# The ninth block's value products: two heads side by side instead of the same rows twice

## The chip, the cores and the metric

The kernel runs on one core of a Trainium2 chip. The metric is the device time of one execution in microseconds; less is better. The profile names the engines PE (TensorE's products), PEld (TensorE's loading of the stationary operand), DVE (VectorE), ACT (ScalarE), POOL (GpSimd) and SP (SyncE, which issues most transfers).

## The reference

Attention over 8 batches, 8 heads, 576 positions and 64 features, followed by a mixture of 8 experts in which each token is sent to one expert. Half of the heads see the last 32 positions, the other half every fourth of the last 128.

```python
scores = scale * np.matmul(q, k.transpose(0, 1, 3, 2))       # (8, 8, 576, 576)
scores = np.where(masks[None], scores, -1e9)                 # 32 allowed positions for each query
attn = np.exp(scores - scores.max(-1)); attn = attn / (attn.sum(-1) + 1e-9)
x = np.matmul(attn, v)                                       # -> (batch, position, 512)
# for each token: e = argmax(x @ w_gate), or the expert of the token before it where a local gate says so
out[b, s] = p[e] * (np.maximum(x[b, s] @ w1[e], 0.0) @ w2[e])
```

All of it is in float32.

## The kernel before

**Blocks.** The 576 positions are nine blocks of 64 queries (`QB`, `NB`). The queries of a block meet 96 keys (`KW`): their own 64 and the 32 before them. The dilated heads are put into the same form by an order of positions that the host applies. Heads go in pairs; there are 32 pairs (`NPB`), and each passes through the same steps.

**Steps of a pair n.** `scores(n)` writes masks and scores with keys on the partitions into two-bank PSUM tiles, in two units of five and four blocks; line 338 (DVE) applies the masks of the second unit, line 340 (ACT) takes the exponentials. `values(n)` multiplies the probabilities by the values, into which a column of ones is joined, so that column 64 of the 65 is the sum of the probabilities. A product has 96 contracted rows, 64 queries and 65 columns, and stands in one half of TensorE's columns: block 2k goes to PSUM partitions 0 to 63, block 2k+1 to partitions 64 to 127. Five slots (`SLOTS`) of two blocks are needed for nine blocks; in the last slot the second half repeats block 8 (`min(2 * k + h, NB - 1)`, line 383), so that all 128 partitions are written. `HALVES` splits the slots into two PSUM tiles `pv`, of two and three slots. For each tile DVE takes the reciprocals of the sums (line 389, into `rec`) and multiplies the 64 features by them (line 390, into `x`).

**Turning and storing.** Two pairs share a tile `x`. `turn(m)` transposes it for the routing: eight transposes of 128 positions (line 406) with two copies on ACT (line 407), then two of the 64 left over (line 410) and one copy (line 412), into `xt`. `store(m)` writes `x` to two tensors `xd` in DRAM, from which the experts later gather rows: one transfer for 512 positions (line 420) and one for the last 64 (line 422). `logits(g)` and the functions after it route a group of two batches on the basis of `xt`.

**Order.** PE, DVE, GpSimd and SP work in the order in which the program is written. In iteration n of the main loop: `scores(n)`, `share` (GpSimd copies the 32 overlapping rows of the values, line 276), a piece of routing work from the list `waiting` (`gap(SHARE)`), `values(n - 1)`, in odd iterations `turn((n - 3) // 2)`, another piece of routing work, then SP's loads for pair n + 3 (lines 264 and 269) and `store((n - 3) // 2)`. Routing work is taken from the list by a fixed credit and not by time. The tiles `pv`, `tp` and those of the routing share four PSUM banks (`banks`); scores have two tiles of two banks. Four sets of keys and values are held (`AHEAD`), three tiles `x`.

`paced(n)` lets GpSimd wait for a reciprocal of pair n before it gathers rows. `check()` looks, late in the expert stage, whether all of the reciprocals in `rec` lie between two bounds; if not, an exact version of the whole is run, which otherwise isn't.

**After attention** come the experts, 152 us to the end: products of weights (lines 923 to 1031), in which TensorE is fed by weights that SP loads one expert after the other.

Of the kernel before, what the change touches and what calls it, by code (L numbers as in the profile page):

```python
# [10 lines left out]
F32 = mybir.dt.float32  # L11
# [4 lines left out]
Alu = mybir.AluOpType  # L16
# [6 lines left out]
P = 128  # L23
B, H, S, DH = 8, 8, 576, 64
D = H * DH
# [7 lines left out]
QB = 64  # L33
NB = S // QB
# [3 lines left out]
NPB = B * NP  # L38
UNITS = ((0, 5), (5, 9))
SLOTS = (NB + 1) // 2  # L40
HALVES = ((0, 2), (2, SLOTS))
CB = 3
# [4 lines left out]
VW = DH + 1  # L47

CH = 2
# [165 lines left out]
def whole(ctx, tc, exact, bad, qk, v, wgl, w1, w2, con, adm, msk, qmk, out, cst, wg, ones, warm):  # L215
# [32 lines left out]
    def bank(shape, name):  # L248
        return banks.tile(shape, F32, name=name, tag="bank")

    rec = once.tile([P, NPB, SLOTS, 2], F32, name="rec")
    pace = once.tile([1, 2], F32, name="pace")
# [18 lines left out]
    def paced(n):  # L271
        nc.gpsimd.tensor_copy(pace, rec[:1, n, SLOTS - 1])

# [97 lines left out]
    def values(n):  # L371

        vt = loaded[n][2]
        if n % 2 == 0:
            xs[n // 2] = xp.tile([P, SLOTS, 2, 2, DH], F32, name="x")
        x = xs[n // 2]
        pr = prob.pop(n)
        for a, z in HALVES:
            pv = bank([P, z - a, 2, VW], "pv")
            for k in range(a, z):  # L380
                for u in range(2):
                    for h in range(2):
                        i = min(2 * k + h, NB - 1)
                        c, p = next((c, p) for c, p in reversed(pr) if c <= i)
                        nc.tensor.matmul(pv[h * QB:(h + 1) * QB, k - a, u], lhsT=p[:, u, (i - c) * QB:(i - c + 1) * QB],  # L385
                                         rhs=vt[:, u, i], start=True, stop=True, tile_position=(0, h * QB),
                                         skip_group_check=True)
            r = rec[:, n, a:z]
            nc.vector.reciprocal(r, pv[:, :, :, DH])
            nc.vector.tensor_tensor(x[:, a:z, n % 2], pv[:, :, :, :DH],  # L390
                                    r.unsqueeze(3).to_broadcast([P, z - a, 2, DH]), op=Alu.mult)
        del loaded[n]

    def turn(m):

        x = xs[m]
        b, g = divmod(m, 2)
# [5 lines left out]
        for c in range(CH):  # L403
# [3 lines left out]
            nc.scalar.copy(xt[:, g, c, s:s + full], tp.rearrange("p k t -> p (k t)"))  # L407
        tp = bank([P, CH, S - full], "tp")
        for c in range(CH):
            nc.tensor.transpose(tp[:, c], x[:S - full, S // P, c].rearrange("p u d -> p (u d)"),  # L410
                                ident[:S - full, :S - full])
        nc.scalar.copy(xt[:, g, :, s + full:s + S], tp)

    def store(m):

        x = xs.pop(m)
        b, g = divmod(m, 2)
        full = S // P * P
        to = xd[g][b * S:(b + 1) * S]
        nc.sync.dma_start(out=to[:full].rearrange("(k p) f -> p k f", p=P),  # L420
                          in_=x[:, :S // P].rearrange("p k g u d -> p k (g u d)"))
        nc.sync.dma_start(out=to[full:], in_=x[:S - full, S // P].rearrange("p g u d -> p (g u d)"))

# [716 lines left out]
    def check():  # L1140

        flat = rec.rearrange("p n k u -> p (n k u)")
        fine = stage.tile([P, D], F32, name="y", bufs=3)[:, :NPB * SLOTS * 2]
        nc.vector.tensor_scalar(fine, flat, 1.0 / HIGH, None, Alu.is_ge)
# [6 lines left out]
        all_fine = sm.tile([1, 1], F32, name="all_fine")  # L1151
        nc.vector.tensor_scalar(all_fine, lp, float(P * NPB * SLOTS * 2), None, Alu.is_lt)
        over = sm.tile([1, 1], F32, name="over_any")
# [133 lines left out]
```

## Time and profile before

| | us |
|---|---|
| median of 3 runs | 668.17 (665.80 to 672.63) |
| the profiled execution | 665.66 |
| its span, first to last instruction | 663.7 |
| first scores; first product of an expert | 6.9; 154.2 |

| engine | busy us | share of the span | instructions |
|---|---|---|---|
| PE | 648.9 | 98% | 6466 |
| DVE | 373.4 | 56% | 755 |
| POOL | 190.7 | 29% | 169 |
| ACT | 189.2 | 28% | 348 |

How to read it: a line of a group names the source line, the engine, the operation, the output and inputs, the partitions by elements, and after x the count; behind the bar are the busy time and the mean duration of one in ns. The groups' busy time is a union, so for products that overlap in the pipeline it is less than count by duration. In the order of time a line has the start, the busy length, and in brackets how long the engine had been idle and what ended it. The clock granted to TensorE was full in every slice (0.999 on average). A float32 product shows as two records, a transpose as one.

### The profile page before, as it was taken

The page shows a single profiled execution, that of the slowest core. Times are in us where ns is not written, and L with a number is a line of the kernel's source. Part 1 is how long each engine was busy: PE and PEld are TensorE (multiplying, and loading weights), DVE is VectorE, ACT ScalarE, POOL GpSimd, SP SyncE. Part 2 cuts the span into 40 slices and gives each one's busy share as a digit, 9 for nine tenths or more (in the row PEclk, how much of TensorE's full clock was granted, in tenths as well). Part 3 has the DMA queues.
Part 4 walks back from the last instruction along what each step waited for, and adds up shares of the span by engine and source line. Part 5 has one row for each costly group of instructions (what it writes and reads, how often), then busy time and mean ns, then how long its engine had stood idle before and what let it go on. Part 6 is the DMA issues. An engine that isn't in the chain of part 4 may idle for free. (4 is left out here: it accounts for less than half of the span.)

```text
span 663.7 us, 15298 instructions
## 1 busy us (share of the span) xinstructions
PE 648.9 (98%) x6466; PEld 570.0 (86%) x6466; DVE 373.4 (56%) x755; ACT 189.2 (28%) x348; POOL 190.7 (29%) x169
## 2 busy tenths in 40 slices
PE   8999999999999999999999999999999999999996
PEld 6988888887688999999599989998899989899893
DVE  3548678584596595373547382717464536547441
ACT  3544343442113331222213223231222222223210
POOL 3322212251025420222551253323144113050021
PEclk9999999999999999999999999999999999999999
DMA  8989899748205398484543456541045451453001
GB/s 317 304 308 317 275 287 312 244 142 317 120 33 191 104 422 332 175 290 169 208 150 132 162 191 226 236 164 48 14 177 214 177 218 61 158 192 144 1 33 49
DMA packets 29357, 126.38 MB, mean 190 GB/s; under 512 B 4221, under 2 KB 13789, under 8 KB 25312
## 3 DMA queue, kind: packets, MB, share of 16 engines
q1 hardware_dynamic: 22480, 106.10, 44.1%
q0 software_dynamic: 6800, 19.21, 8.5%
q8 instruction: 53, 0.87, 0.5%
q14 instruction: 24, 0.20, 0.1%
HBM read 142.07 MB, written 19.20 MB: 243 GB/s over the span
## 5 line engine op out<-in xcount | busy, mean ns | idle before, releaser
L977 POOL DMA_INDIRECT out_dram<-y,tok x36 | 57.4, 1595 | 290.9 <-DVE y L1046 121.0
L949 PE MATMUL hp<-xc,sum 128*128 128x128 f32 x720 | 85.6, 275 | 0.4 <-DVE sum L816 0.4
L949 PEld LDWEIGHTS hp<-xc,sum 128*128 128x128 f32 x720 | 82.8, 192 | 0.8 <-PE hp L949 0.5
L1031 PE MATMUL yp<-sum,hc 128*128 128x256 f32 x360 | 82.7, 379 | 0.0
L959 DVE TENSOR_TENSOR h<-hp,h 128x512 f32<-128x512 f32 x45 | 30.9, 690 | 90.8 <-PE hp L949 90.1
L1031 PEld LDWEIGHTS yp<-sum,hc 128*128 128x128 f32 x360 | 68.2, 190 | 9.6 <-ACT y L1039 0.3
L1046 DVE SCALAR_TENSOR_TENSOR y<-yp,gate,y 128x256 f32<-128x256 f32 x45 | 21.7, 482 | 75.1 <-issue 48.0
L276 POOL COPY vt<-vt 32x1040 f32<-32x1040 f32 x32 | 35.5, 1110 | 93.0 <-DMA vt<-in_v_dram 62.1
L949 PE MATMUL hp<-xe,raw 128*128 128x128 f32 x480 | 58.8, 276 | 0.0
L949 PEld LDWEIGHTS hp<-xe,raw 128*128 128x128 f32 x480 | 56.6, 192 | 1.8 <-issue 1.5
L1031 PE MATMUL yp<-raw,h 128*128 128x256 f32 x240 | 57.0, 380 | 0.0
L333 PE MATMUL two<-kq 64*96 64x64 f32 x1152 | 54.9, 245 | 0.0
L853 POOL DMA_INDIRECT xg<-xd,tok x40 | 45.7, 1143 | 27.6 <-PE hp L949 15.0
L333 PEld LDWEIGHTS two<-kq 64*96 64x96 f32 x1152 | 52.8, 162 | 0.0
L1031 PEld LDWEIGHTS yp<-raw,h 128*128 128x128 f32 x240 | 44.4, 190 | 5.5
L953 ACT COPY h<-hp 128x512 f32<-128x512 f32 x45 | 26.4, 587 | 79.2 <-PE hp L949 75.3
L960 ACT ACTIVATE h<-h 128x512 f32<-128x512 f32 x45 | 28.4, 632 | 67.2 <-DVE h L959 67.2
L853 POOL DMA_INDIRECT xg<-xd,pos x40 | 43.9, 1098 | 12.1 <-issue 11.1
L338 DVE SCALAR_TENSOR_TENSOR pr<-two,mk 96x512 f32<-96x512 f32 x32 | 21.9, 685 | 44.9 <-ACT pr L340 34.0
L385 PE MATMUL pv<-vt,pr 96*64 96x65 f32 x1280 | 44.6, 224 | 0.8 <-issue 0.8
L385 PEld LDWEIGHTS pv<-vt,pr 96*64 96x64 f32 x1280 | 40.0, 138 | 3.3 <-issue 1.5
L1039 ACT ACTIVATE y<-yp,gate 128x256 f32<-128x256 f32 x45 | 21.3, 476 | 55.8 <-PE yp L1031 48.5
(223 smaller groups left out, 1008.7 us busy)
## 6 DMA issues: line engine op xcount, KB each, us to landing
raw<-in_w_dram SPq DMA_DIRECT2D x48, 2048.0 KB
kq<-in_qk_dram SPq DMA_DIRECT2D x32, 592.0 KB
vt<-in_v_dram SPq DMA_DIRECT2D x32, 292.5 KB
xd<-x SPq DMA_DIRECT2D x16, 512.0 KB
raw<-in_w_dram SPq DMA_DIRECT2D x4, 512.0 KB
xd<-x SPq DMA_DIRECT2D x16, 64.0 KB
xg<-xd,tok POOLq DMA_INDIRECT x40, 3.2
xg<-xd,pos POOLq DMA_INDIRECT x40, 3.2
```

The costliest lines, as they stand in the source:

```text
L276: nc.gpsimd.tensor_copy(vt[:WIN, :, 1:], vt[QB:, :, :NB - 1])
L333: nc.tensor.matmul(sc[:KW, u, (i - a) * QB:(i - a + 1) * QB], lhsT=kt[h, i * QB:i * QB + KW], rhs=qt[h, i * QB:(i + 1) * QB], start=bool(a ...
L338: nc.vector.scalar_tensor_tensor(pr, sc[:KW, :, :w], -CEIL, mk[:, kind].unsqueeze(1).to_broadcast([KW, 2, w]), Alu.max, Alu.min)
L385: nc.tensor.matmul(pv[h * QB:(h + 1) * QB, k - a, u], lhsT=p[:, u, (i - c) * QB:(i - c + 1) * QB], rhs=vt[:, u, i], start=True, stop=True, ...
L853: nc.gpsimd.indirect_dma_start(out=x[:rows, g], out_offset=None, in_=xd[g] if units[u]["late"] else xd[g][:EARLY * GS], in_offset=bass.Ind ...
L949: nc.tensor.matmul(to[:, m], lhsT=a[:, m, kk], rhs=b[:, kk], start=first and m == 0 and kk == 0, stop=(kk == DK // 2 - 1), skip_group_chec ...
L953: nc.scalar.copy(at((0, 1, 3)[k]), of)
L959: nc.vector.tensor_tensor(at(k), of, at(k), op=Alu.add)
L960: nc.scalar.activation(at(k), at(k), Act.Relu)
L977: nc.gpsimd.indirect_dma_start(out=out, out_offset=bass.IndirectOffsetOnAxis(ap=of_unit(u, "tok", j), axis=0), in_=y, in_offset=None, boun ...
L1031: nc.tensor.matmul(to, lhsT=a[:, m], rhs=b[:, m], start=first and m == 0, stop=(m == FK // 2 - 1), skip_group_check=True)
L1046: nc.vector.scalar_tensor_tensor(at(k), of, of_unit(u, "gate", k // 2), at(k), Alu.mult, Alu.add)
```

## The change

The ninth block is no longer written twice. Its two heads stand side by side in the two halves of the columns: head 0 in partitions 0 to 63, head 1 in partitions 64 to 127, of one further column group in the second `pv` tile. So each pair has nine column groups of sums in place of ten, and 18 products in place of 20. What follows is fitted to that layout: `rec` has nine columns (`SUMS`); the last group is multiplied by its own instruction, which writes it twice, into both head positions of a part `end` of the tile `x`; `turn` transposes `end` with all 128 rows, and takes the two wanted quarters of the result by two copies; `store` writes the last 64 positions with one transfer for each head.

```diff
-SLOTS = (NB + 1) // 2
-HALVES = ((0, 2), (2, SLOTS))
+FULLS = S // P
+HALVES = ((0, 2), (2, FULLS))
+SUMS = NB
...
-    rec = once.tile([P, NPB, SLOTS, 2], F32, name="rec")
+    rec = once.tile([P, NPB, SUMS], F32, name="rec")
...
-        nc.gpsimd.tensor_copy(pace, rec[:1, n, SLOTS - 1])
+        nc.gpsimd.tensor_copy(pace, rec[:1, n, SUMS - 2:])
...
-            xs[n // 2] = xp.tile([P, SLOTS, 2, 2, DH], F32, name="x")
-        x = xs[n // 2]
+            x = xp.tile([P, 4 * (FULLS + 1) * DH], F32, name="x")
+            xs[n // 2] = (x[:, :4 * FULLS * DH].rearrange("p (k g u d) -> p k g u d", k=FULLS, g=2, u=2),
+                          x[:, 4 * FULLS * DH:].rearrange("p (g u d) -> p g u d", g=2, u=2))
+        x, end = xs[n // 2]
         pr = prob.pop(n)
+
+        def product(to, h, u, i):
+            c, p = next((c, p) for c, p in reversed(pr) if c <= i)
+            nc.tensor.matmul(to[h * QB:(h + 1) * QB], lhsT=p[:, u, (i - c) * QB:(i - c + 1) * QB],
+                             rhs=vt[:, u, i], start=True, stop=True, tile_position=(0, h * QB), skip_group_check=True)
+
         for a, z in HALVES:
-            pv = bank([P, z - a, 2, VW], "pv")
+            last = z == FULLS
+            w = 2 * (z - a)
+            pv = bank([P, w + last, VW], "pv")
             for k in range(a, z):
                 for u in range(2):
                     for h in range(2):
-                        i = min(2 * k + h, NB - 1)
...
+                        product(pv[:, 2 * (k - a) + u], h, u, 2 * k + h)
+            if last:
+                for u in range(2):
+                    product(pv[:, w], u, u, NB - 1)
-            r = rec[:, n, a:z]
-            nc.vector.reciprocal(r, pv[:, :, :, DH])
-            nc.vector.tensor_tensor(x[:, a:z, n % 2], pv[:, :, :, :DH],
-                                    r.unsqueeze(3).to_broadcast([P, z - a, 2, DH]), op=Alu.mult)
+            r = rec[:, n, 2 * a:2 * z + last]
+            nc.vector.reciprocal(r, pv[:, :, DH])
+            nc.vector.tensor_tensor(x[:, a:z, n % 2], pv[:, :w, :DH].rearrange("p (k u) d -> p k u d", u=2),
+                                    r[:, :w].rearrange("p (k u) -> p k u", u=2).unsqueeze(3).to_broadcast(
+                                        [P, z - a, 2, DH]), op=Alu.mult)
+            if last:
+                nc.vector.tensor_scalar(end[:, n % 2], pv[:, w:, :DH].to_broadcast([P, 2, DH]), r[:, w:], None, Alu.mult)
...
-        tp = bank([P, CH, S - full], "tp")
+        tp = bank([P, CH, P], "tp")
         for c in range(CH):
-            nc.tensor.transpose(tp[:, c], x[:S - full, S // P, c].rearrange("p u d -> p (u d)"),
-                                ident[:S - full, :S - full])
-        nc.scalar.copy(xt[:, g, :, s + full:s + S], tp)
+            nc.tensor.transpose(tp[:, c], end[:, c].rearrange("p u d -> p (u d)"), ident)
+        for u in range(2):
+            h = slice(u * DH, (u + 1) * DH)
+            nc.scalar.copy(xt[h, g, :, s + full:s + S], tp[h, :, h])
...
-        nc.sync.dma_start(out=to[full:], in_=x[:S - full, S // P].rearrange("p g u d -> p (g u d)"))
+        for u in range(2):
+            nc.sync.dma_start(out=to[full:].rearrange("t (g u d) -> t u g d", g=2, u=2)[:, u],
+                              in_=end[u * DH:(u + 1) * DH, :, 0])
...
-        fine = stage.tile([P, D], F32, name="y", bufs=3)[:, :NPB * SLOTS * 2]
+        fine = stage.tile([P, D], F32, name="y", bufs=3)[:, :NPB * SUMS]
```

## The prediction

> **What bounds the kernel now.** I read the page's busy shares first, then TensorE's waits, then the groups by shape, then the order of time in the attention stage, which is the only stage that the change touches (about 7 to 154 us of a span of 663.7).
>
> ```profile
> PE 648.9 (98%) x6466; PEld 570.0 (86%) x6466; DVE 373.4 (56%) x755; ACT 189.2 (28%) x348; POOL 190.7 (29%) x169
> L385 PE MATMUL pv<-vt,pr 96*64 96x65 f32 x1280 | 44.6, 224 | 0.8 <-issue 0.8
> ```
>
> TensorE is busy for 98% of the span, and its waits are few: the longest total that it waits for anything is 1.7 us. So what TensorE no longer does in attention brings the whole end forward, unless another engine is late there. The second line is the value products: 1280 records for 32 head pairs are 40 per pair, two for each of 20 float32 products. The page hides where VectorE is not at 56%. Two stretches show it, an ordinary turn (33.50 on) and one that routes tokens (55.10 on); columns after the length are PE, PEld, DVE, ACT, POOL, clock, DMA share, GB/s:
>
> ```profile
> 33.50:40.82 7.32, 7.32 (x173) 6.88 (x170) 3.90 (x11) 3.91 (x7) 2.09 (x2) 1.00 0.99 352
> 55.10:72.23 17.13, 15.96 (x347) 14.71 (x346) 16.20 (x45) 7.72 (x15) 5.45 (x4) 1.00 0.96 307
> ```
>
> In the first TensorE never pauses and VectorE has half its time free. In the second VectorE is busy 95% and TensorE loses 1.2 us. That difference decides this case.
>
> **TensorE: what goes.** The order of time in an ordinary stretch:
>
> ```profile
> 40.02 1.39 PE L385 MATMUL pv<-vt,pr 96*64 96x65 f32 x40
> 41.34 1.09 PE L406 MATMUL tp<-cst,x 128*128 128x128 f32 x8
> 42.36 0.33 PE L410 MATMUL tp<-cst,x 64*128 64x64 f32 x2
> 42.62 2.15 PE L439 MATMUL lp<-xt,wg 128*32 128x288 f32 x32
> ...
> 35.04 0.27 PE L410 MATMUL tp<-cst,x 64*128 64x64 f32 x1
> 35.05 0.33 PE L326 MATMUL two<-am 64*96 64x320 bf16 x1
> ```
>
> One product record lasts 0.22 us, so 40 in 1.39 us start (1.39-0.22)/39 = 0.030 us apart. The ninth block loses two products, four records: 4 x 0.030 = 0.119 us per head pair (unrounded spacing 0.0297), 32 times = **-3.8 us**. The rest of the 1.32 us to the next row is a tail that stays. That the two halves of the new pair keep this pace is read from the rows before: those too alternate between column halves.
>
> **TensorE: the turned remainder.** The two remainder transposes have 64 rows; they become 128x128 like the eight before them. Those start (1.09-0.28)/7 = 0.116 us apart. Now the ten take 41.34 to 42.62 = 1.28 us; ten alike take 9 x 0.116 plus the 0.20 us that follow the eighth now, 1.25. So nothing in a turn followed by other work. But in five turns (20, 27, 35, 108, 119 us) the small transposes run among the mask products of the next scores, as the last two rows show. There the turn from L406 to the next values takes 2.92 us (34.02 to 36.94); afterwards 1.25 plus an even turn's 1.76 (38.26 to 40.02) = 3.01. Five times 0.1 = **+0.5**. Bounds: -0.5 (0.03 saved in each of 16) to +1.6 (0.1 lost in each); I take the value counted by turn.
>
> The trace has 0.20 us between the eighth large transpose's start and the first small one, twice their pace. [...]
>
> **VectorE: what is added.** Durations by shape:
>
> ```profile
> L390 DVE TENSOR_TENSOR x<-pv,rec 128x384 f32<-128x384 f32 x32 | 17.8, 557 | 1.1
> L390 DVE TENSOR_TENSOR x<-pv,rec 128x256 f32<-128x256 f32 x32 | 13.6, 425 | 1.1
> L389 DVE RECIPROCAL rec<-pv 128x6 f32<-128x6 f32 x32 | 6.1, 191 | 0.4 <-PE pv L385 0.2
> L389 DVE RECIPROCAL rec<-pv 128x4 f32<-128x4 f32 x32 | 5.4, 168 | 0.0
> L998 DVE TENSOR_SCALAR y<-yp,gate x4: 349/351/479, 360.8 to 609.9; 128x128 f32<-128x128 f32 x3, 128x256 f32<-128x256 f32 x1
> ```
>
> The second multiplication shrinks from 384 to 256 elements: -0.132 us. Its reciprocal has 5 values in place of 6: -0.011. The new tensor_scalar writes 128x128 from PSUM with a scalar per partition; L998 is the same shape and operands: +0.350, and about 0.03 between two VectorE instructions. Together +0.237 us a head pair, 7.6 us in all. (Bounds of the new instruction: 0.255, L453's 96x108 without a scalar tensor, to 0.57, L503's slowest 12x96 beside a GpSimd copy; L998 matches in shape.)
>
> In ordinary turns the cover is VectorE's idle time ahead of L338, 1.1 to 4.5 us. In the routing stretches there is none:
>
> ```profile
> 66.75 0.56 DVE L390 TENSOR_TENSOR x<-pv,rec 128x384 f32<-128x384 f32 x1
> 67.22 0.94 DVE L573 TENSOR_TENSOR lane<-cst,lanes 96x768 f32<-96x768 f32 x1
> ...
> 69.66 0.42 DVE L390 TENSOR_TENSOR x<-pv,rec 128x256 f32<-128x256 f32 x1
> 70.23 0.30 PE L410 MATMUL tp<-cst,x 64*128 64x64 f32 x2 [0.92 <-DVE rec L389]
> ```
>
> TensorE waits for the multiplication at 69.66 to free a bank. Behind it are three head pairs (57.02, 61.21, 66.75) in a VectorE run with 0.13 us of idle time: 3 x 0.237 - 0.13 = +0.6 at that point, and the 4 x 0.119 = 0.5 that TensorE had gained since 55.10 are lost to the same wait. **+1.1.** The group from 93 to 112 us has 1.2 us of small VectorE gaps for four pairs' 0.95, but 0.8 of it comes from one TensorE pause at 102.7 that nothing explains: +0.3. The tail (143 to 152) ends on the last x: its path gains 0.24 from the pair before, loses 0.14 and adds 0.38, ends some 0.2 later, and two pairs' gain (0.24) is lost: +0.4. One more 0.1 for the third group near 111.
>
> **What is covered.** ACT gets a second remainder copy (L412's row: 0.28 us, 16 times). It lies ahead of the next exponentials, where ACT is idle 0.49 us in the tightest ordinary turn; without that cover the exponentials come 0.28 us later, at most 4.5 us in all. SP issues one more transfer a turn, 0.51 us by L422, ahead of the next key load; SP then waits for value products (L269, 59.8 us over 27 times). The stores become 256-byte pieces: 256 in place of 64 packets of 1 KB. By the trace's packets those last 46 ns, 512-byte ones 27, 64-byte ones 11. At 27 this is 256 x 27 - 64 x 46 = 4.0 us on 16 engines, 0.25 us a turn; at 46, 0.55. Bounds are 11 and 46 and I take 27, the nearest size. Keys (packets of 4,736 bytes) land 1.9 us or more ahead of their scores before the first store, 3.9 or more after it. So nothing. The check reads 288 reciprocals in place of 320, and the GpSimd pace copy waits for a reciprocal as before: nothing.
>
> [...]
>
> **The sum.** -3.8 + 0.5 + 1.1 + 0.3 + 0.4 + 0.1 = **-1.4 us**. The profiled execution took 665.66 us, 2 more than its span, so it would take 664.3. The runs' median is 668.17, 2.5 above; the change goes one for one to the end, since the expert stage too is TensorE's: 668.2 - 1.4 = **666.8**. That is no change that a measurement of this kernel would tell from none (about 1%, 6.7 us).
>
> **Rivals.**
> 1. *The gain arrives whole.* For it: TensorE waits little, and the wait at 70.23 follows a 1.05 us cast that a GpSimd copy had slowed, which need not recur. Then -3.8, 664.4.
> 2. *VectorE becomes the bound; slower.* A head pair inside a saturated run turns -0.119 into +0.237, a swing of 0.356. The net gain of 3.3 is gone at 3.3/0.356 = 9.3 of 32 pairs. My count above is about 6. VectorE has no gap over 0.5 us in 53-74, 93-115 and 140-152 and little in the two 7 us runs at 47 and 85: 16 pairs in all, which gives -3.3 + 16 x 0.356 = +2.4, 670.6. Against it: TensorE reads most of these results a turn later.
> 3. *The change does not do what it says on TensorE:* the four records were free beside their neighbours, and the pass keeps 1.3 us. Then only costs stay: +2.4 from the sum's other terms, 670.6. Against it: the even spacing of starts.
> 4. *Small packets bind.* DMA is already 96 to 99% busy in both stretches above. It decides when three stores eat the 3.9 us of lead, 1.3 us each: 0.19 + 1.3 = 1.49 us for 256 packets on 16 engines, 93 ns a packet, twice the 1 KB packet's 46. At 140 ns, +2.05 us a turn is 33 us of transfers against some 16 idle (11% of 146): +17 less the gain, some 682.
>
> **Chances.** Forecast 0.52, rival 1 0.16, rival 2 0.18, rival 3 0.08, rival 4 0.06. None but rival 4 leaves the 1%; the runs spread 6.8 us, which gives 0.04 for faster and 0.02 more for slower. So 0.04, 0.88, 0.08. The range holds rivals 1 to 3 and reaches 2.4 us below and 1.4 above them for the spread of the runs: 662.0 to 672.0.
>
> **What would show it.** L385 with 36 records and about 1.27 us a pass; ten equal transposes; L998's kind of row in values at 0.35 us, 32 times; VectorE up about 7.6 us; a longer wait of the transposes near 70 us. Wrong if the stage's end (now 154.2) moves by more than 4 us, if TensorE begins to wait for VectorE in ordinary turns, or if keys land late.

## The result, and the profile after

The changed kernel took 667.69 us (median of 22 runs, 664.97 to 675.34), the kernel before 666.15 (22 runs beside it). The ratio is 1.001, with a 95% interval from 0.9992 to 1.0028: 0.5 us faster to 1.9 us slower, no change that counts. The forecast of no change holds, but its ratio, 0.998 (1.4 us faster), lies just outside the interval. The profiled execution took 668.03 us with a span of 666.2. In some runs the clock granted to TensorE is lower on average and the run is up to 15 us longer (e3's slowest, 681.11 at 0.977, beside 666.38 at full clock); where a text below says "at full clock", only runs with a mean granted clock of 0.997 or more are in the median (a run with one fall of 3.4 us in attention still counts: e11's profiled one has 0.997): 667.04 for the change (19 runs) and 666.09 for the kernel before (20; its clocks are not on record, and the two runs near 672.6 are left out by their time), 0.95 us slower.

The page of the changed kernel, its span, its busy shares and the value products:

```profile
span 666.2 us, 15143 instructions
...
PE 647.0 (97%) x6338; PEld 567.3 (85%) x6338; DVE 376.3 (56%) x787; ACT 192.9 (29%) x364; POOL 187.5 (28%) x169
...
L384 PE MATMUL pv<-vt,pr 96*64 96x65 f32 x1152 | 40.9, 225 | 0.3 <-issue 0.3
```

There are 128 value records fewer, 36 per pair in place of 40, each as long as before. Yet the span is 2.5 us longer. The attention stage, from the first scores to the first product of an expert, went from 147.30 (6.89 to 154.19) to 148.09 (6.89 to 154.98): +0.79. The rest of the span, from there to TensorE's last product, went from 503.23 to 504.79. The clock has no part in these 1.6 us: in both traces it falls only behind that last product, at 662.4 and 662.7 us. Waits make 1.0 of it, 0.57 us for a gather of rows of `xd` and 0.48 for ACT. For that gather e1, e3, e9 and e11 wait 0.46 to 0.57 us too, and the kernel before, e2, e4 and e10 wait 0 to 0.19; so the change may have a small part in the expert stage, which no run took apart.

What is to be explained is the stage: +0.79 where -1.4 was forecast, near the 0.95 at full clock. The +0.79 itself holds some luck. Each trace has a pause of TensorE that nothing releases (last section): it lengthens a pass of values by 1.07 us in the kernel before and by 0.57 in the changed one. Without the two the difference would be +1.3 (an estimate).

The groups by shape, with mean durations in ns behind the comma:

```profile
L400 DVE TENSOR_TENSOR x<-pv,rec 128x256 f32<-128x256 f32 x64 | 27.2, 425 | 2.2
L404 DVE TENSOR_SCALAR x<-pv,rec 128x128 f32<-128x128 f32 x32 | 10.9, 342 | 0.0
L399 DVE RECIPROCAL rec<-pv 128x5 f32<-128x5 f32 x32 | 5.9, 184 | 0.0
L426 ACT COPY xt<-tp 64x128 f32<-64x128 f32 x32 | 8.3, 261 | 2.2 <-PE tp L423 1.9
L423 PE MATMUL tp<-cst,x 128*128 128x128 f32 x32 | 6.5, 284 | 4.6 <-DVE rec L399 3.5 <-ACT xt L420 1.0
```

The added multiplication (L404) takes 0.342 us; 0.350 had been taken from L998. The durations of VectorE's instructions in the stage add up to 115.8 us in place of 108.6, 7.2 more. Its busy time rose by less than half of that, from 99.3 to 102.4 us (on the page from 373.4 to 376.3), since the records overlap: behind a multiplication of `pv` the next instruction starts 0.08 us before the end. The last line is where the time went: the remainder transposes now wait 3.5 us for VectorE's reciprocals and multiplications. TensorE's waits say how often:

```profile
PE tp L423 <- DVE rec L399: 3.5, 4, 1.2
...
PE kp L562 <- DVE x L400: 0.6, 1, 0.6
PE tp L884 <- DMA xg<-xd,tok: 0.6, 1, 0.6
PE hp L939 <- ACT le L459: 0.5, 1, 0.5
PE yp L1047 <- ACT y L1055: 0.5, 1, 0.5
```

Before, the first of these was one wait of 0.9 us, the second one of 0.4, and the others did not exist. The third and the last lie in the expert stage. Laid out along the stage, with a stretch measured from the start of one pass of values to the start of another:

| stretch | before | after | difference | forecast |
|---|---|---|---|---|
| first scores to the first pass | 4.47 | 4.61 | +0.14 | 0 |
| pairs 0 to 9 (ordinary turns) | 39.10 | 38.23 | -0.86 | -0.9 |
| pair 10 (turn at 51 us) | 4.64 | 5.63 | **+1.00** | -0.1 |
| pairs 11 to 14 | 17.14 | 17.33 | +0.20 | +0.6 |
| pairs 15 to 18 | 20.96 | 20.76 | -0.20 | -0.5 |
| pairs 19 to 22 | 17.58 | 17.25 | -0.33 | -0.1 |
| pairs 23 to 27 | 24.40 | 24.10 | -0.30 | -0.4 |
| pair 28 (turn at 136 us) | 4.77 | 5.47 | **+0.70** | -0.1 |
| pairs 29 to 31, to the first expert | 14.25 | 14.70 | +0.45 | 0.0 |

The forecast column is the prediction's sum, shared out by place. In pairs 0 to 9, where nothing waits, the sum is right to 0.1 us; in pairs 15 to 18 it is 0.3 too good. The row of pairs 19 to 22 holds both pauses: without them it would be about +0.2 (an estimate), since the turn at 107 us now waits 0.59 us for VectorE. The sum fails most at two single turns that it had counted as covered, and at the stage's end. The order of time in the first of them, in the changed kernel (start, length, and in brackets the idle time before it):

```profile
49.73 1.27 PE L384 MATMUL pv<-vt,pr 96*64 96x65 f32 x36
...
49.79 0.42 DVE L400 TENSOR_TENSOR x<-pv,rec 128x256 f32<-128x256 f32 x1
50.13 0.34 DVE L404 TENSOR_SCALAR x<-pv,rec 128x128 f32<-128x128 f32 x1
50.39 0.68 DVE L339 SCALAR_TENSOR_TENSOR pr<-two,mk 96x512 f32<-96x512 f32 x1
50.93 1.09 PE L419 MATMUL tp<-cst,x 128*128 128x128 f32 x8
...
51.11 1.05 POOL L277 COPY vt<-vt 32x1040 f32<-32x1040 f32 x1 [3.45 <-PE pv L384]
51.26 1.10 DVE L502 TENSOR_TENSOR_SCAN run<-row 12x96 f32<-12x96 f32 x1
...
52.47 0.42 DVE L400 TENSOR_TENSOR x<-pv,rec 128x256 f32<-128x256 f32 x1
...
53.04 0.41 PE L423 MATMUL tp<-cst,x 128*128 128x128 f32 x2 [1.01 <-DVE rec L399]
```

and in the kernel before:

```profile
50.26 0.56 DVE L390 TENSOR_TENSOR x<-pv,rec 128x384 f32<-128x384 f32 x1
50.73 0.68 DVE L338 SCALAR_TENSOR_TENSOR pr<-two,mk 96x512 f32<-96x512 f32 x1
...
51.60 0.34 DVE L486 TENSOR_TENSOR_SCAN run<-row 12x96 f32<-12x96 f32 x1
...
51.86 1.05 POOL L276 COPY vt<-vt 32x1040 f32<-32x1040 f32 x1 [4.25 <-PE pv L385]
```

Before, the scan starts 0.26 us ahead of GpSimd's copy and takes 0.34. In the changed kernel the copy starts first, 0.15 ahead, and the scan takes 1.10. The copy starts when the pass of values ends (51.85 before, 51.00 after), so TensorE's own gain brings it forward by 0.75; the scan comes forward by only 0.34. VectorE's queue there begins 0.62 earlier than before (the masks, 46.80 and 46.18), and loses 0.15 at L479, which takes 0.40 us in place of 0.25 beside the copy of the pair before, and 0.12 to the new multiplication. These 0.12 are seen in the rows: from the start of the second multiplication to that of the masks it is 0.47 us before (50.26 to 50.73) and 0.60 now (49.79 to 50.39). With the reciprocal, which is a little shorter, it is 0.121 us (0.696 and 0.817, the medians of the pairs in which VectorE goes on without a gap). Behind the scan stand the multiplications that free the PSUM bank for L423. At 136 us the copy is first in both kernels: 0.85 ahead of the scan before, which takes 0.41, and 0.43 ahead in the changed one (135.88 and 136.31), where the scan takes 0.82.

The end of the stage:

```profile
152.31 2.15 PE L455 MATMUL lp<-xt,wg 128*32 128x288 f32 x32
154.53 0.40 ACT L459 COPY le<-lp 128x288 f32<-128x288 f32 x1 [1.31 <-PE lp L455]
154.98 1.35 PE L939 MATMUL hp<-xe,raw 128*128 128x256 f32 x5 [0.52 <-ACT le L459]
```

The first expert product waits for ACT's copy of the last logits, which it doesn't read; before it followed the logits without a gap (152.11 to 154.19). That the two tiles got the same PSUM bank in the changed program and different ones in the one before is a guess; no trace shows the banks. The wait is there in e1, e5 and e12 too, and in none of the other runs below.

### The profile page after: what moved, and what is told of

Read it like the earlier page. It is cut to its first block, busy times and chain, and to the rows that moved or that the text cites. A ratio compares the mean times of both kernels' runs of the same rounds, so it can differ in the third digit from the quotient of the medians.

```text
span 666.2 us, 15143 instructions
## 1 busy us (share of the span) xinstructions
PE 647.0 (97%) x6338; PEld 567.3 (85%) x6338; DVE 376.3 (56%) x787; ACT 192.9 (29%) x364; POOL 187.5 (28%) x169
## 2 busy tenths in 40 slices
DMA packets 32686, 126.38 MB, mean 190 GB/s; under 512 B 8573, under 2 KB 17117, under 8 KB 28640
## 5 line engine op out<-in xcount | busy, mean ns | idle before, releaser
L993 POOL DMA_INDIRECT out_dram<-y,tok x36 | 55.4, 1539 | 295.4 <-DVE y L1062 124.1
L975 DVE TENSOR_TENSOR h<-hp,h 128x512 f32<-128x512 f32 x45 | 30.9, 690 | 90.9 <-PE hp L965 90.9
L384 PE MATMUL pv<-vt,pr 96*64 96x65 f32 x1152 | 40.9, 225 | 0.3 <-issue 0.3
L384 PEld LDWEIGHTS pv<-vt,pr 96*64 96x64 f32 x1152 | 36.4, 138 | 2.8 <-issue 0.9
```

What stands on the lines that cost most here:

```text
L384: nc.tensor.matmul(to[h * QB:(h + 1) * QB], lhsT=p[:, u, (i - c) * QB:(i - c + 1) * QB], rhs=vt[:, u, i], start=True, stop=True, tile_posi ...
L975: nc.vector.tensor_tensor(at(k), of, at(k), op=Alu.add)
L993: nc.gpsimd.indirect_dma_start(out=out, out_offset=bass.IndirectOffsetOnAxis(ap=of_unit(u, "tok", j), axis=0), in_=y, in_offset=None, boun ...
```

## The experiments

Theory A: the gain is eaten where GpSimd's copies slow VectorE's instructions, and would be whole without them. Theory B: VectorE's load as such, where it runs without a gap, makes TensorE wait. The times, each beside the kernel before on the same chip; "full clock" is the median at full clock less that of the kernel before, with the number of runs; "stage" is the attention stage of one profiled execution, "VectorE" the sum of the durations of its instructions there:

| run | time | ratio to before, 95% | full clock | stage | VectorE |
|---|---|---|---|---|---|
| before | | | | 147.30 | 108.6 |
| the change | 667.69 | 1.0010 [0.9992, 1.0028] | +0.95 (19) | 148.09 | 115.8 |
| e1_act9 | 665.86 | 0.9986 [0.9966, 1.0007] | -1.1 (11) | 146.21 | 104.6 |
| e2_before_dose | 673.22 | 1.0116 [1.0067, 1.0166] | +1.7 (1) | 150.49 | 120.0 |
| e3_after_dose | 672.14 | 1.0023 [0.9978, 1.0067] | -0.6 (5) | 154.72, clock | 127.6 |
| e4_once | 665.64 | 0.9994 [0.9968, 1.0019] | -1.3 (10) | 147.25 | 107.3 |
| e5_after_ns | 668.74 | 0.9983 [0.9958, 1.0009] | -0.4 (12) | 146.57 | 111.6 |
| e6_before_ns | 668.04 | 0.9997 [0.9985, 1.0008] | -1.1 (11) | 145.74 | 105.2 |
| e7_after_vf | 674.04 | 1.0085 [1.0062, 1.0108] | (0) | 152.62, clock | 113.0 |
| e8_act9_vf | 670.98 | 1.0022 [0.9998, 1.0045] | -1.7 (2) | 149.46, clock | 105.2 |
| e9_after_late | 665.60 | 0.9987 [0.9964, 1.0009] | -1.2 (10) | 146.50 | 115.8 |
| e10_before_late | 666.26 | 1.0002 [0.9979, 1.0026] | -1.6 (9) | 146.54 | 108.5 |
| e11_act9_late | 664.67 | 0.9986 [0.9971, 1.0000] | -2.0 (10) | 145.86, clock | 105.2 |
| e12_two_copies | 669.91 | 1.0031 [1.0002, 1.0060] | +1.1 (9) | 148.48 | 115.1 |

In the stages marked "clock" the granted clock fell to half on the way. A single stage also holds pauses of TensorE that lengthen it by up to 1.3 us and differ from trace to trace (last section), so stages less than about 1 us apart say little without the stretches behind them.

### e1_act9: the ninth multiplication on ACT

```diff
-                nc.vector.tensor_scalar(end[:, n % 2], pv[:, w:, :DH].to_broadcast([P, 2, DH]), r[:, w:], None, Alu.mult)
+                nc.scalar.activation(end[:, n % 2], pv[:, w:, :DH].to_broadcast([P, 2, DH]), Act.Copy, scale=r[:, w:])
```

> The changed kernel, with the ninth block's multiplication on ACT in place of VectorE (an activation with the reciprocal as its scale); nothing else differs. Theory 1, VectorE: the 3.8 us that TensorE saves are real and are lost only where VectorE's added 0.34 us a pair stands in a run without gaps. Then VectorE has 0.14 us a pair less than in the kernel before, TensorE's waits for it fall to or under those of before, and the time is 2.5 to 3.5 us under the kernel before (ratio 0.995 to 0.996). Theory 2, the rest of the change: full-height transposes, the second ACT copy and the 256-byte stores eat the gain. Then the time stays within 1 us of the kernel before, as the change has it, or above it, since ACT gets about 9 us more.

The stage is 1.9 us shorter than the changed kernel's and 1.1 shorter than before's; the time is 0.9 us under before by the ratio (interval 2.3 under to 0.5 over) and 1.1 at full clock. Right in direction, though the interval reaches past 0, and under half in size. The two turns make up the 1.9: pair 10 takes 4.52 in place of 5.63, pair 28 4.74 in place of 5.47; the other stretches differ by -0.23 to +0.46 and cancel. In the order of time the scan is ahead of the copy again:

```profile
50.22 0.35 DVE L502 TENSOR_TENSOR_SCAN run<-row 12x96 f32<-12x96 f32 x1
...
50.48 1.05 POOL L277 COPY vt<-vt 32x1040 f32<-32x1040 f32 x1 [3.64 <-PE pv L384]
```

What is still lost has other owners: the wait at the stage's end is the same, a turn at 104 us waits 1.1, and the last pair now reaches its values before GpSimd has copied them:

```profile
PE tp L423 <- DVE rec L399: 1.9, 2, 1.1
...
PE pv L384 <- POOL vt L277: 0.8, 1, 0.8
```

### e2_before_dose and e3_after_dose: one more multiplication per pair

Each adds, behind the second multiplication, a spare one of the added kind, whose result nobody reads; here in the changed kernel, and alike in the kernel before:

```diff
+                spare = work.tile([P, 2, DH], F32, name="spare")
+                nc.vector.tensor_scalar(spare, pv[:, w:, :DH].to_broadcast([P, 2, DH]), r[:, w:], None, Alu.mult)
```

> The kernel before, with the one VectorE instruction that the change adds (a tensor_scalar of 128x128 from PSUM with a reciprocal as its scalar) put behind the second multiplication of every pair, into a spare tile that nobody reads. VectorE has 0.37 us a pair more, 12 us in all; products, transposes and stores are as before. Theory 1: the time grows by 3 to 6 us (ratio 1.005 to 1.009), as waits of TensorE in the four routing groups. Theory 2: VectorE has the room, under 1 us.

The stage went from 147.30 to 150.49, +3.2. A pause in the pass at 89.7 us that nothing released makes 1.3 of it, but the pause of the kernel before, 1.07, is missing; so some 3.0 is left (an estimate), at the low end of what was expected, where the one run at full clock has +1.7. The passes of values kept their 1.32 us, so VectorE's load alone brings waits like those of the change:

```profile
PE tp L414 <- DVE rec L389: 3.3, 4, 1.3
```

Before there was 0.9 of them. Pair 10 alone loses 0.89, and there the scan meets the copy:

```profile
51.85 1.05 POOL L276 COPY vt<-vt 32x1040 f32<-32x1040 f32 x1 [4.06 <-DMA vt<-in_v_dram]
51.88 1.23 DVE L490 TENSOR_TENSOR_SCAN run<-row 12x96 f32<-12x96 f32 x1
```

The ratio, 1.0116, is mostly that of runs with a fallen clock, five of six; what that has to do with the waits is told in the last section.

> The changed kernel with its added VectorE instruction issued twice, the second time into a spare tile that nobody reads: 0.37 us a pair more again. Theory 1: 4 to 7 us above the changed kernel (ratio to the kernel before 1.006 to 1.011), more per dose than in the kernel before since TensorE is shorter. Theory 2: under 1 us above the changed kernel.

The stage rose by 6.6, and that number must not be taken as it stands. The stretches of 5 us from 70 us on (the last three columns are granted clock, DMA share and GB/s):

```profile
70.00:75.00 5.00, 3.75 (x42) 3.36 (x42) 3.64 (x9) 1.76 (x5) 0.87 (x1) 0.64 0.91 332
75.00:80.00 5.00, 5.00 (x51) 4.88 (x50) 2.43 (x7) 0.63 (x1) 0.17 (x1) 0.50 0.30 90
80.00:85.00 5.00, 5.00 (x87) 4.80 (x85) 1.07 (x3) 0.91 (x2) 1.04 (x1) 0.84 0.26 105
```

(1 - 0.64) + (1 - 0.50) + (1 - 0.84) = 1.02 times 5 us are 5.1 us of clock, so that about 1.5 is left, 1.2 of it in the same stretches. The five runs at full clock are 0.6 under the kernel before beside them, where the change is 0.95 over its own. So at full clock 11.8 us more of VectorE's durations on top of the change cost between nothing and 1.5 us: a miss for 4 to 7. The median of all 12 runs, though, is 4.9 over the kernel before; seven of them are not at full clock. In pairs 0 to 9 the stretch is the same to 0.01 us. Theory B, read as a price per us of load, falls, as far as the clock is full. What the load did bring is one wait of 2.67 us, from 68.6, right ahead of the clock's fall.

### e4_once: the ninth block written once

The whole second tile of sums is multiplied by one instruction of 128x320 (0.49 us), and the remainder is turned by eight products in column halves:

```diff
-                nc.vector.tensor_scalar(end[:, n % 2], pv[:, w:, :DH].to_broadcast([P, 2, DH]), r[:, w:], None, Alu.mult)
...
+            nc.vector.tensor_tensor(x[:, n % 2, 2 * a:2 * z + last], pv[:, :, :DH],
+                                    r.unsqueeze(2).to_broadcast([P, w + last, DH]), op=Alu.mult)
...
-            nc.tensor.transpose(tp[:, c], end[:, c].rearrange("p u d -> p (u d)"), ident)
+            for u in range(2):
+                h = slice(u * DH, (u + 1) * DH)
+                nc.tensor.matmul(tp[h, c], lhsT=x[:, c, SUMS - 1], rhs=ident[:, h], start=True, stop=True,
+                                 tile_position=(0, u * DH), skip_group_check=True)
```

> The ninth block's heads side by side as in the change, but written once: a tile of nine column groups for each pair, so that one multiplication of 128x320 takes the ninth group too (about 0.49 us, against 0.557 before and 0.425 + 0.342 in the change), and the remainder is turned by four products with a half of the identity, each in its half of the columns, which gives the layout of before and needs one ACT copy. The stores are smaller still: 1024 packets of 512 bytes and 256 of 256 a turn, four transfers. Theory 1: VectorE has 0.07 us a pair less than before, TensorE keeps its 3.8 us and loses at most 0.1 us a turn on eight records in place of two; 2 to 4 us under the kernel before (ratio 0.994 to 0.997). A rival, small packets: the same time as the kernel before or above it.

A miss: VectorE is down to 107.3, under before's 108.6, and the stage is still 147.25, the time within the interval of no change. A turn takes 1.02 + 0.38 us, where the changed kernel's takes 0.93 + 0.31 to 0.40; a pause of 1.0 in the pass at 32.0 us is in it (the kernel before's trace has one as long), and pair 28 lost 0.74 to a wait for VectorE: there the scan starts 0.24 behind the copy and takes 1.01. So a lighter VectorE does not do it by itself: it depends on where its instructions fall. At full clock the time is 1.3 under before. The stores of this kernel have the smallest pieces of all, and in attention no product waited for a transfer.

### e5_after_ns and e6_before_ns: without GpSimd's copies

Both leave out the copies from pair 4 on, as told in the expectation; their routing differs from the reference's, so they are read against each other:

```diff
-            share(k)
+            if k < AHEAD:
+                share(k)
```

> The changed kernel without the GpSimd copies of the overlapping value rows from pair 4 on (the rows of an earlier pair stay in their place, so values and routing are not the reference's; the check's verdict is set to 'fine' so that the exact version isn't run). To be read against e6, which has the same data. Theory A, collisions: in the traces so far every VectorE instruction of attention that lasts 0.1 us longer than its shortest like stands beside one of these copies (4.4 us of lengthening in the changed kernel, 3.3 before). If that is what ate the gain, the attention stage (first scores to first expert product) is 2.5 to 3.5 us shorter here than in e6. Theory B, VectorE's plain load and place in the order: the stage here is within 1 us of e6, or longer.

> The kernel before, without the same copies and with the same check left out; the partner of e5. Theory A: the stage is 1 us shorter than the 147.3 of the kernel before at most, since TensorE waits little there, and 2.5 to 3.5 us longer than e5. Theory B: within 1 us of e5.

Without the copies both stages are about 1.5 us shorter. The difference between the layouts is the same as with them, +0.83 against +0.79 (at full clock 0.7 and 0.95), and not 2.5 to 3.5 the other way, so Theory A falls as an account of the whole sum. But the sum hides three parts. Pairs 10 and 28 differ by +0.09 and +0.05 in place of +1.00 and +0.70: their loss is gone with the copies. The pauses differ: e6 has none, and e5 has one like the changed kernel's; without them the layouts would differ by +1.3 with the copies and +0.3 without (estimates), so that the like size of +0.79 and +0.83 is partly chance. And up to the last logits the changed layout is 0.74 us ahead. It is given back, and more, at the stage's end, where the wait for ACT's copy has grown:

```profile
PE hp L939 <- ACT le L459: 1.5, 1, 1.5
```

### e7_after_vf and e8_act9_vf: values' multiplications ahead of routing

The first piece of routing work goes behind the values in place of ahead of them, so that the bank is freed earlier; e8 has the multiplication of e1, too.

```diff
-        gap(SHARE)
         if 1 <= n <= NPB:
             values(n - 1)
+        gap(SHARE)
```

> The changed kernel, with the iteration's first piece of routing work put behind the value products instead of ahead of them; nothing is added or taken away. VectorE then multiplies the first value tile, whose bank the third tile of the turn waits for, ahead of that piece. Theory B: TensorE's waits in the turns (1.17 near 51 us, 1.08 more than an ordinary turn near 68, 0.75 near 107, 0.88 near 136) mostly go, and the stage falls from 148.1 to 144.5 to 146 us; the time is 2 to 4 us under the changed kernel and 1 to 3 under the kernel before (ratio 0.9955 to 0.9985). Theory A: the waits stay within 1 us of what they were, since the collisions are untouched.

> Both: the ninth multiplication on ACT (as in e1, which had a stage of 146.2 us) and the routing piece behind the values. Theory B: a stage of 143.5 to 145 us, since TensorE's products alone would allow 147.3 - 3.8 and the waits of the kernel before (some 2 us) go as well; 2.5 to 4 us under the kernel before (ratio 0.994 to 0.9965). Theory A: 146, as e1.

The stages, 152.62 and 149.46, are far above what was expected, and much of it is the clock: in e7 it was at half at 56.5 to 63.3 and at 145.3 to 152.1 us, in e8 at 142.9 to 149.7. Half of these lengths is 6.8 and 3.4 us, without which some 145.8 and 146.0 would be left (an estimate), the first within what was expected and the second not. The two runs of e8 at full clock are 1.7 under before; of e7's six none was. The waits have moved: the routing is a chain of round trips between TensorE and VectorE, and these are now late,

```profile
PE cp L524 <- DVE run L519: 3.5, 3, 1.4
```

and two of e7's three waits stand right ahead of the clock's falls. As versions both are worse or no better; that the order of the work as such costs time is not shown.

### e9_after_late, e10_before_late, e11_act9_late: the remainder turned later

The remainder transposes and their copies leave the turn for the following iteration, behind its values, except at the end of a group; there their bank has long been free. In e9, by its expectation, the last logits and the first expert tile have different banks; in none of the three does the first expert product wait for the copy. The same lines in each:

```diff
+        if n >= 4 and n % 2 == 0 and (n - 4) // 2 in ends:
+            turn_end((n - 4) // 2)
         if n >= 3 and n % 2 == 1:
             turn((n - 3) // 2)
```

> Changed kernel; the two remainder transposes of a turn (and their two copies) are taken out of the turn and written behind the value products of the following iteration, except where a group of two batches ends. They then take a PSUM bank that has long been free, so TensorE should not wait there for VectorE's multiplication. In this program the last logits tile and the first expert tile lie in different banks, too. Theory B (the gain is lost where TensorE waits for VectorE to free the bank of the remainder transposes, and at the stage's end where the first expert product takes the bank of the last logits): the attention stage, 148.1 in the changed kernel, goes to 144.5-146, and the time to 2-4 under the kernel before. Rival (VectorE is saturated in those stretches and is waited for in another place anyway): stage 147-148.5, time the same as the changed kernel's.

The stage is 146.50, 1.6 us less, between the two expectations, and the time is 0.9 under before by the ratio, short of 2 to 4. The waits of the remainder transposes are gone. At 51 us the scan was again 0.03 behind the copy:

```profile
51.37 1.04 POOL L277 COPY vt<-vt 32x1040 f32<-32x1040 f32 x1 [4.11 <-PE pv L384]
51.40 1.23 DVE L513 TENSOR_TENSOR_SCAN run<-row 12x96 f32<-12x96 f32 x1
...
53.30 0.17 PE L519 MATMUL last<-cst,run 12*1 12x12 f32 x1 [0.99 <-DVE rec L399]
```

and now the product that needs the scan itself waits 0.99 us. The wait has only a new name, as the rival had it for this place. Two passes near the end wait for GpSimd's copies (0.51 and 0.93 us).

> Kernel before with the same move of the remainder transposes, without the changed value products. If the move is worth something only because the change loads VectorE, the stage stays at 146.5-147.5 (147.3 in the kernel before) and the time within 1 of it. If the move is a gain by itself, about 1 (its one wait of 0.9 us there and two of 0.3), the stage is 145.5-146.5, and the changed layout's own gain is what lies between this run and the one with the changed kernel: 0.5-2 us by theory B, 0 or less by the rival.

146.54: the move gains 0.8 us in the kernel before too, and with it the changed layout stands where the old one does (146.50; at full clock it is 0.4 slower). By stretches, e9 against e10: -0.75 in pairs 0 to 9, +0.95 and +0.52 in pairs 10 and 28, +1.28 at the end. -0.04 is the sum, but a pause of 0.9 at 88.3 us in e10 is part of it.

> As the changed kernel with the moved remainder, and the ninth group's multiplication on ACT in place of VectorE (VectorE's added 7 us are gone and 4 more). If what stays lost in the moved version is VectorE's load, the stage goes 0.5-1.5 us lower still, to 143.5-145.5, the time 2.5-4.5 under the kernel before. If the move alone has taken all the waits, it equals the moved version within 0.5; ACT's added load could cost up to 0.5 where the exponentials are late.

The stage is 145.86, 0.6 under the moved version, with the clock at half from 146.5 to 149.9 us, 1.7 us' worth; without that it would be about 144.2 (an estimate), within what was expected. The time, 664.67, is the lowest, at full clock 2.0 under before (663.73 to 667.30 against 664.59 to 668.71): the two parts, the lighter VectorE and the moved transposes (1.1 and 1.2 by themselves), add up roughly, and fall short of the 2.5 to 4.5 expected. By the interval, 0 to 1.9 us, it is at best 0.3% faster than the kernel before, which is no change by this kernel's measure.

### e12_two_copies: two copies left out

As e5, but only the two copies that met the scans. Missing value rows of two pairs change which tokens go to which expert, so that only the attention stage is read.

```diff
-            share(k)
+            if k not in (13, 29):
+                share(k)
```

> Changed kernel without two of GpSimd's 32 copies of overlapping value rows: those of pairs 13 and 29, which in the changed kernel run at 51.1 and 135.9 beside VectorE's scan (1.10 and 0.82 in place of 0.34). Left out with them: the branch into the exact version at the end; the outputs of the two pairs' heads are not the reference's. Theory A' (at these two turns, and there only, the prediction's cover fails because the scan is slowed by the copy): the stretches between one pass of values and the next, 5.63 from 49.7 and 5.47 from 134.8, go to 4.5-4.8 each; the stage goes from 148.1 to 146.2-146.8, the time to 0.7-2 under the changed kernel. Rival (VectorE has too much queued in these turns with or without the slow scan): the stretches keep 5.2 or more, the stage 147.5-148.3.

The turn at 51 us, in the order of time:

```profile
51.17 1.09 PE L419 MATMUL tp<-cst,x 128*128 128x128 f32 x8
...
51.39 0.34 DVE L502 TENSOR_TENSOR_SCAN run<-row 12x96 f32<-12x96 f32 x1
...
52.41 0.41 PE L423 MATMUL tp<-cst,x 128*128 128x128 f32 x2
```

The scan takes 0.34 again and the stretch of pair 10 goes from 5.63 to 4.77, as Theory A' had it: the copy cost 0.86 there. That of pair 28 goes from 5.47 to 5.01, half of what was expected; 0.24 of a wait for VectorE stays. The stage did not follow, 148.48: pairs 0 to 9 took 1.5 us longer than in the changed kernel's trace, with two pauses that nothing released among it, and the wait at the end grew by 0.94, as in e5. Nor did the time, 1.1 over before at full clock. So the cause at pair 10 is shown, at pair 28 for about two thirds of its 0.70, and the stage as a whole is not repaired by it.

The other traces agree at pair 10. Where the copy starts first its stretch is 5.63 (the change), 5.53 (e2) and 5.27 (e9); where the scan does it is 4.64 (before), 4.52 (e1), 4.60 (e4), 4.33 (e10) and 4.21 (e11). One trace differs: in e3, with the most load, the scan starts 0.39 ahead of the copy and the stretch is still 5.42.

## Why the prediction was right or wrong, point by point

**The forecast** of no change was right. That says little of the mechanism, since by the prediction itself no rival but the last leaves the 1%. Its size, -1.4 us, was not right: the stage lengthened by 0.79, and the runs' ratio excludes -1.4 narrowly.

**TensorE, what goes (-3.8).** Right to the hundredth: the pass of values went from 1.32 to 1.20 us in every ordinary pair, 0.12 each. Rival 3 is out.

**The turned remainder (+0.5).** Right: the turn from the first transpose to the next values takes 3.01 us where it took 2.92 (33.51 to 36.52, before 34.02 to 36.94), and 0.1 more in the two other early turns that were named; those at 108 and 119 us grew by 0.87 and 0.23, the first through its wait for VectorE. The wait between transposes of different size is gone as well: from the eighth to the first of the remainder it is 0.11 us where it was 0.20.

**VectorE, what is added (0.237 a pair).** The duration of the new instruction was right, and the added durations, 7.2 us against 7.6. But what VectorE is held longer is 0.121 us a pair, 3.9 in all, half of the term. "About 0.03 between two VectorE instructions" holds behind a reciprocal; behind a multiplication of `pv` the next instruction starts 0.08 before the end, as the prediction's own rows have it (66.75 + 0.56 is 67.31, and the next starts at 67.22).

**Group at 55 to 72 us (+1.1).** The mechanism was right (L423 waits 1.19 us in place of 0.92, with the same three pairs ahead of it), the size too large: the stretch lost 0.7 against its share of the gain, of which 0.3 is a wait of another product (L524, at 57 us). With 0.121 in place of 0.237 the prediction's own sum for the wait, 3 x 0.121 - 0.13, is 0.23, close to the 0.27 by which it grew. For pairs 19 to 22 +0.3 was forecast and 0.1 measured, or some 0.5 without the two pauses; for the third group 0.1 and 0.2.

**The failed step** is "In ordinary turns the cover is VectorE's idle time ahead of L338", applied to every turn outside the named stretches. The turns at 51 and 136 us each have one piece of routing in VectorE's queue ahead of the multiplications. The idle time there covers the new multiplication, but not a scan that a copy holds up for 0.5 to 0.8 us. In the trace of before that scan was 0.26 us from the meeting, and what decides the meeting stood in the sum: the copy is released by the end of a pass that the change brings forward, the scan stands behind the instruction that it adds. That VectorE waits for GpSimd at all was no term of the sum. e12 and e5 give the price at 51 us, 0.86 and 0.91 of the 1.00; at 136 us it is 0.46 and 0.65 of the 0.70, the rest being VectorE's queue. Together the two turns are 1.9 of the 2.2 us between forecast and trace.

**The tail (+0.4).** Its net loss was 0.45 where 0.0 was forecast. Of it 0.52 is the wait for the copy of the last logits, for which the prediction had no step. In e9 to e11 it is gone; but they differ in the moved transposes too, so its price by itself was not tried.

Without the two meetings (1.84 by e1) and that wait (0.52) the trace's +0.79 would be -1.6, near the forecast -1.4. That nearness is partly luck: 0.5 of it is the difference of the two pauses, and the VectorE term was twice too large.

**Rival 2, VectorE as the bound.** Its sign came true and its mechanism didn't: e3 loads VectorE with 11.8 us more of durations for 0 to 1.5 us at full clock. Not 16 pairs in saturated runs, but two single turns and the end. **Rival 1**, the gain whole, is what e11 comes nearest to, 2.0 at full clock. **Rival 3** is out by the passes. **Rival 4** is out too: packets under 512 bytes went from 4,221 to 8,573, and the keys' least lead behind the first store from 3.9 to 3.4 us. The 4,096 packets of 256 bytes that the change brings lasted 18 ns each (median), less than the 27 that the prediction took from 512-byte packets and far from the 93 at which this rival begins to bind; no run shows the 140 behind its 682 us.

What stays open: what e11 still lacks from the 3.3 us that TensorE saves net. Its last passes wait 0.92 us for a GpSimd copy; no run took that away alone.

## What to carry to other kernels

When the bound engine is made faster by 0.1 us a step, list the instructions of two other engines that must not meet and note how far they stand apart: what the faster engine releases comes forward, what stands behind added work does so less (here by 0.75 and 0.34 us), and 0.26 us are used up after a few steps; check cover at each place with its own queue, not by an average turn. Compare, too, the waits at the seams of stages, since an edit far away can bring a new one there. Take what an instruction costs from start to start in rows without a gap, since its duration can overlap the next one (here by 0.08 us). And look at the granted clock of a stretch before its length is read: the largest difference of this study, 6.6 us in e3, was mostly clock (5.1 us).

## What the runs showed of the hardware that was not expected

**Who starts first decides.** The scan (12x96) and GpSimd's copy (32x1040) in the traces: with the scan first, by 0.26 us at 51 us in the kernel before and in e1, it takes 0.34 to 0.35 and the copy 1.05. With the copy first the scan ends 0.20 to 0.22 us after the copy's end, whatever the overlap, in all eight such meetings of the traces: 52.36 against 52.16 and 137.13 against 136.92 in the changed kernel, 52.63 against 52.41 in e9, 136.85 against 136.63 in the kernel before. So its end follows the end of the copy, not the length of the overlap (0.19 us at 136 us in the kernel before, 0.90 at 51 us in the changed one), as if it stood until the copy is done. For the scan the traces show this in one direction alone: with the scan first, by 0.11 to 0.33 us, the copy took 1.05 to 1.08 us, hardly longer than the 1.04 to 1.05 of most others. Three more of the kernel before took 1.48 to 1.87 us (65.1, 69.0 and 109.1 us), beside VectorE's L573, L583 and L589. The multiplications of `pv` were not stretched: in the changed kernel 27 of them lay beside such a copy and took 0.42 (L400) or 0.34 us (L404), as the others did.

**Pauses of TensorE that nothing releases.** In eight of the fourteen attention stages there are one or two, with TensorE idle for 0.14 to 1.02 us in the middle of its work: 0.80 in the kernel before at 102.7, 0.30 in the changed one at 105.7, 0.74 in e4 at 33.1, 1.02 in e2 at 90.9. A pass of values is lengthened by some 0.3 more than the idle time (1.07 for 0.80, 0.57 for 0.30). In all of them TensorE resumes 1.2 to 1.5 us after a 16 KB packet of the instruction queue has ended. But there are 22 or 23 such packets in a stage, and most are followed by no pause. Whether the two belong together no run tested.

**Half the clock shortly behind a pause.** The order of time in e8, each stretch with its length, the busy times of PE, PEld, DVE, ACT and POOL, granted clock, DMA share and GB/s:

```profile
137.00:140.30 3.30, 3.30 (x81) 3.05 (x80) 1.07 (x4) 1.71 (x5) 2.19 (x3) 1.00 0.02 5
140.30:141.70 1.40, 0.01 (x1) 0.00 (x0) 1.25 (x5) 0.32 (x2) 0.00 (x0) 1.00 0.32 94
141.70:142.90 1.20, 1.14 (x25) 1.13 (x27) 0.88 (x4) 0.21 (x1) 1.04 (x1) 1.00 0.42 142
143.00:149.70 6.70, 6.70 (x72) 6.29 (x72) 3.47 (x13) 3.19 (x7) 2.23 (x4) 0.50 0.32 86
149.90:153.00 3.10, 2.86 (x51) 2.56 (x48) 2.79 (x13) 1.20 (x3) 0.19 (x2) 1.00 0.03 11
```

TensorE waits 1.46 us for the routing, works on, and 1.1 us later its clock halves for 6.8 us, in which it is busy all the time. The same order stands ahead of every fall in the attention stages of the traces: pauses of 0.92 (e11), 1.07 and 1.37 (e7), 1.46 (e8) and 2.67 us (e3), and 0.2 to 1.5 us after their end a half clock for 3.4, 6.8, 6.8, 6.8 and 10.2 us: one, two and three times 3.4. But a pause need not bring it: 1.19 in the changed kernel, 1.30 in e2, 1.46 in e12 and 1.5 in e5 did not. Over all runs, a mean clock under 0.997 came in 5 of 6 for e2, 7 of 12 for e3, 6 of 6 for e7 and 10 of 12 for e8, in 3 of 22 for the change, in 0 to 3 of 11 or 12 for the others, and in 8, 3, 3 and 1 of 29, 29, 29 and 17 for the kernel before beside them. Why one pause is followed by half the clock and another is not, the traces do not show. No run varied a pause alone.

**A late copy.** In e5 and e12 ACT began the copy of the last logits about 1.0 us after their end (in e12 at 153.90, the products ended at 152.89), with nothing else on ACT; in the changed kernel it was 0.07. In e6 and e7 the copy was 0.7 and 0.9 late, with no wait behind it. The cause was not found.
